# A linear-attention and MLP block on one core: attention output by tile with DMA transposes

## The chip, the cores and the metric

The kernel runs on one core of a Trainium2 chip. The metric is device time in microseconds; less is better. Engines are named as in the profile: TensorE (PE, its weight loads PEld), VectorE (DVE), ScalarE (ACT), GpSimd (POOL) and SyncE (SP), whose queue issues every DMA of this kernel.

## The reference

x has 2048 rows (tokens) of 576 bf16 values. Four layers follow one another, A, B, A, B, each added to x:

```
x = x + A(layernorm(x), wqkv, wo)      # linear attention, 32 heads of 18
x = x + B(layernorm(x), w1, b1, w2, b2)  # MLP, 576 -> 4608 -> 576

A: q, k, v = y @ wqkv;  phi(t) = where(t > 0, t + 1, exp(t)) + 1e-6
   kv = sum over tokens of phi(k)^T v,  z = sum over tokens of phi(k)   (per head)
   o = (phi(q) @ kv) / (phi(q) . z + 1e-6);   return o @ wo
B: layernorm again, h = gelu(y @ w1 + b1), return h @ w2 + b2
```

## The kernel before, in words

The tokens are 16 tiles of 128 rows. A Tile scheduler orders each engine's instructions; helper functions add dependencies that fix the order of TensorE's matmuls and of the first loads. All weights stay in SBUF. `x` between layers is kept in DRAM (`x_d`) in float32 and loaded again for each residual and layer norm.

**Layer norm** (`LNPipe`, lines 215 to 298) is a pipeline of steps, one per tick: load, statistics on VectorE (L242 to L253), rstd by a power on GpSimd (L258), the normed row tile `y_ring` on VectorE, GpSimd or ScalarE (L270, L274), for a layer B a copy of the last 64 columns beside them (L278), then five TensorE transposes (L287) into PSUM and one copy into `yT` (L289, L291). `yT` holds the transposed rows, 5 blocks of 128 columns by 2048 tokens, and every product of the layer reads it. All 64 tiles of the four layers go this way.

**Layer A, kv stage** (L348 to L403): for each tile the K projection (L356), phi on it (ScalarE exp and shift, L309 and L311, then VectorE, L312 and L314), the V projection (L364, L367) and the accumulation of kv (L380), which also sums phi(k) through a column of ones. From tile 4 on one block of Q, 126 columns by 512 tokens, is projected per tile (L386) and given phi; there are 20 blocks. In the first layer A the layer norm of the tiles runs in the same loop, as do the loads of the MLP weights; masks for the heads are built on GpSimd in the middle of it (L70 to L98).

**Layer A, output stage** (L405 on): the masked kv (L408, L412) is multiplied by `wo` for each of 5 groups of heads (L430). The denominators of 512 tokens are computed by small products (L442, L446), inverted on VectorE (L450), spread to the heads by a product (L458), copied by ScalarE (L460) and multiplied into phi(q) (L462, VectorE, some on GpSimd). Then ten products per tile give the layer's output (L470), the residual is added on VectorE (L336), stored to `x_d` (L341), and for the first four tiles the layer norm of layer B is started.

**Layer B** (`LayerB`, L516 on): in four chunks of 512 tokens. Nine groups of four hidden blocks (L569, gelu by ScalarE, L565) make the hidden layer, in which matmuls of the upper and the lower 64 rows run in pairs; then four tiles of 72 products with `w2` (L616). Residuals are fetched ahead (`prefetch_xo`), the bias is added to them on GpSimd (L326). During a chunk the layer norm of the next chunk's tiles, or at the end that of the next layer A, runs beside it; its transposes stand between the `w2` products.

SP's queue issues DMAs in order, and an instruction that waits on it holds up those behind it.

Of the kernel before, what the change touches and what calls it, by code (L numbers as in the profile page):

```python
# [14 lines left out]
S, D, F, H, DH = 2048, 576, 4608, 32, 18  # L15
P = 128
NT = S // P
KD = 5
# [17 lines left out]
def build(tc, A_x, A_wqkv, A_wo, B_w1, B_b1, B_w2, B_b2, out, dbg=None, n_layers=4):  # L36
    nc = tc.nc
    dbg = dbg or {}
    with ExitStack() as ctx:
        const = ctx.enter_context(tc.tile_pool(name="const", bufs=1))  # L40
        ps_h = ctx.enter_context(tc.tile_pool(name="ps_h", bufs=3, space=PSUM))
        ps_tp = ctx.enter_context(tc.tile_pool(name="ps_tp", bufs=1, space=PSUM))
        ps_acc = ctx.enter_context(tc.tile_pool(name="ps_acc", bufs=1, space=PSUM))
        dpool = ctx.enter_context(tc.tile_pool(name="dram", bufs=1, space=DRAM))

        x_in = A_x.flatten_outer_dims()
        out_f = out.flatten_outer_dims()

# [10 lines left out]
        maskz = const.tile([P, 7, DH], F32, name="maskz")  # L59
        head_sel = const.tile([P, G, H], BF16, name="head_sel")  # L60
        head_bc = const.tile([P, G, P], BF16, name="head_bc")
        quad_mask = const.tile([P, 4, P], BF16, name="quad_mask")
        z_row = const.tile([P, 1], BF16, name="z_row")
        eps_row = const.tile([1, H], BF16, name="eps_row")
        one_row = const.tile([1, P], BF16, name="one_row")

        def build_masks(after):
            sel = nc.gpsimd.affine_select

            def fill(tile_, value):  # L70
                tc.add_manual_dep(nc.gpsimd.memset(tile_[:], value).ins, after, NOSYNC, reason="masks are not urgent")

            fill(maskz, 1.0)
            sel(out=maskz[:], in_=maskz[:], compare_op=ALU.is_ge, fill=0.0,
                base=0, pattern=[[-DH, 7], [0, DH]], channel_multiplier=1)
            sel(out=maskz[:], in_=maskz[:], compare_op=ALU.is_ge, fill=0.0,
                base=DH - 1, pattern=[[DH, 7], [0, DH]], channel_multiplier=-1)
            sel(out=maskz[:], in_=maskz[:], compare_op=ALU.not_equal, fill=1.0,
                base=-126, pattern=[[0, 7], [0, DH]], channel_multiplier=1)
            fill(z_row, 0.0)  # L80
            fill(eps_row, 1e-6)
            fill(one_row, 1.0)
            sel(out=z_row[:], in_=z_row[:], compare_op=ALU.not_equal, fill=1.0,
                base=-126, pattern=[[0, 1]], channel_multiplier=1)
            fill(head_sel, 1.0)
            sel(out=head_sel[:], in_=head_sel[:], compare_op=ALU.is_ge, fill=0.0,
                base=0, pattern=[[126, G], [-DH, H]], channel_multiplier=1)
            sel(out=head_sel[:], in_=head_sel[:], compare_op=ALU.is_ge, fill=0.0,
                base=DH - 1, pattern=[[-126, G], [DH, H]], channel_multiplier=-1)
            fill(quad_mask, 1.0)  # L90
            sel(out=quad_mask[:], in_=quad_mask[:], compare_op=ALU.is_ge, fill=0.0,
                base=0, pattern=[[-32, 4], [0, P]], channel_multiplier=1)
            sel(out=quad_mask[:], in_=quad_mask[:], compare_op=ALU.is_ge, fill=0.0,
                base=31, pattern=[[32, 4], [0, P]], channel_multiplier=-1)
            fill(head_bc, 0.0)
            hb = head_bc[:, :, 0:126].rearrange("p g (h d) -> p g h d", h=7)
            for quad in range(4):
                sel(out=hb, in_=hb, compare_op=ALU.not_equal, fill=1.0,  # L98
                    base=-32 * quad, pattern=[[-7, G], [-1, 7], [0, DH]], channel_multiplier=1)

        wqkv_sb = const.tile([P, KD, 3 * D], BF16, name="wqkv_sb")
        wo_sb = const.tile([126, G, D], BF16, name="wo_sb")
# [4 lines left out]
        b2_bc = const.tile([P, D], BF16, name="b2_bc")  # L107
        yT = const.tile([P, KD, S], BF16, name="yT")
        kvT = const.tile([P, G, 126], BF16, name="kvT")
        zsel = const.tile([P, G, H], BF16, name="zsel")  # L110
        NY = 4
        y_ring = [const.tile([P, DPAD], BF16, name=f"y_ring{i}") for i in range(NY)]
        NV = 3
        v_ring = [const.tile([P, G, P], BF16, name=f"v_ring{i}") for i in range(NV)]
        x_d = dpool.tile([NT, P, D], F32, name="x_d")

        work = ctx.enter_context(tc.tile_pool(name="work", bufs=2))
        blk = ctx.enter_context(tc.tile_pool(name="blk", bufs=NF))

        x0_tiles = {}  # L120

        NOSYNC = mybir.DependencyInfo(mybir.DependencyClass.NoSync, mybir.DependencyReason.SCHED_ONLY)
        SYNC = mybir.DependencyInfo(mybir.DependencyClass.Sync, mybir.DependencyReason.DATA)
        relay_sb = const.tile([P, 2], F32, name="relay_sb")
        nc.gpsimd.memset(relay_sb[:], 0.0)
        chain = dict(last=None)

        def chained(inst):
            if chain["last"] is not None:
                tc.add_manual_dep(inst.ins, chain["last"], NOSYNC, reason="start-up DMA issue order")  # L130
            chain["last"] = inst.ins.name
            return inst

        pe_chain = dict(on=False, last=None)

        def pe(inst):
            if pe_chain["on"]:
                if pe_chain["last"] is not None:
                    tc.add_manual_dep(inst.ins, pe_chain["last"], NOSYNC, reason="TensorE order in the MLP")
                pe_chain["last"] = inst.ins.name  # L140
            return inst

        def load_x0(t):
            x0 = blk.tile([P, D], BF16, name="x0", tag="blk")
            chained(nc.sync.dma_start(out=x0[:], in_=x_in[t * P:(t + 1) * P, :]))
            x0_tiles[t] = x0

        def load_wqkv(part):
            cols = slice(part * D, (part + 1) * D)
            chained(nc.sync.dma_start(out=wqkv_sb[:, 0:4, cols],  # L150
                                      in_=A_wqkv[0:4 * P, cols].rearrange("(k p) n -> p k n", p=P)))
            chained(nc.sync.dma_start(out=wqkv_sb[0:64, 4, cols], in_=A_wqkv[4 * P:D, cols]))

        load_x0(0)
        load_x0(1)
        load_wqkv(1)
        load_x0(2)
        load_x0(3)
        load_wqkv(2)
        load_x0(4)  # L160
        for i in (NY - 1, 0, 1, 2):
            nc.vector.memset(y_ring[i][:], 0.0)
        warm_ps = ps_h.tile([P, 512], F32, name="warm_ps", tag="h")
        for i in range(NWARM):
            nc.tensor.matmul(warm_ps[:], lhsT=y_ring[NY - 1][:, 0:P], rhs=y_ring[NY - 1][:, 0:512], start=True, stop=True)
        act_dummy = const.tile([P, 1], F32, name="act_dummy")
        nc.scalar.activation(out=act_dummy[:, 0:1], in_=neg_half[:, 0:1], func=ACT.Exp)
        nc.vector.memset(wqkv_sb[64:P, 4, :], 0.0)
        for vr in v_ring:
            nc.gpsimd.memset(vr[:, 4, 72:126], 0.0)  # L170
            nc.gpsimd.memset(vr[:, :, 126:127], 1.0)
            nc.gpsimd.memset(vr[:, :, 127:128], 0.0)

        def late_setup():
            build_masks(pool_last["norm"])

        def piece_wo():
            chained(nc.sync.dma_start(out=wo_sb[:, 0:4, :], in_=A_wo[0:504, :].rearrange("(g p) n -> p g n", p=126)))
            chained(nc.sync.dma_start(out=wo_sb[0:72, 4, :], in_=A_wo[504:D, :]))
# [10 lines left out]
        def piece_w2(i):  # L190
            chained(nc.sync.dma_start(out=w2_sb[:, 6 * i:6 * (i + 1), :],
                                      in_=B_w2[6 * i * P:6 * (i + 1) * P, :].rearrange("(f p) d -> p f d", p=P)))
# [3 lines left out]
        def piece_b1_dma():  # L196
# [4 lines left out]

        def piece_b2_dma():
            chained(nc.sync.dma_start(out=b2_bc[:], in_=B_b2.partition_broadcast(P)))

        def bias_casts():
            nc.vector.tensor_copy(out=b1T[:], in_=bias_stage.pop("b1")[:])

        late_pieces = [piece_wo, piece_b1_dma] + [(lambda i=i: piece_w1(i)) for i in range(9)] + \
                      [(lambda i=i: piece_w2(i)) for i in range(6)]
        late_pads = [late_setup]  # L210

        state = dict(ycnt=0, vcnt=0)
        pool_last = dict(norm=None)
        dve_last = dict(norm=None)

        class LNPipe:
            def __init__(self):
# [7 lines left out]
            def busy(self):  # L225
                return len(self.items)
# [501 lines left out]
```

## Time and profile before

| | us |
|---|---|
| median of 3 runs (808.61 to 811.14) | 810.84 |
| span of the profiled execution | 809.3 |
| first layer A: kv stage and Q until the last accumulation | 0 to 77.2 |
| first layer A: output stage | 77.2 to 124.0 |
| first layer B | 124.0 to 413.4 |
| second layer A: kv stage | 413.4 to 471.3 |
| second layer A: output stage | 471.3 to 520.4 |
| second layer B and the last store | 520.4 to 809.3 |

The profile has no other time of the profiled execution than its span; the runs lie about 1.5 us above it. A row such as `L470 PE MATMUL wo_ps<-kvwo,pq 126*128 126x288 bf16 x256 | 43.8, 297` names the line, the engine, the tiles written and read, the shapes and the count, then the busy time together and the mean of one in ns. Matmuls overlap, so their mean is longer than what one adds; the chain of work gives what a run of them adds. In a row of the stretches the numbers after the length are the busy times of PE, PEld, DVE, ACT and POOL, with the count of instructions in brackets, then the granted TensorE clock, the busy share of the DMA engines and GB/s.

### The profile page before, as it was taken

The page shows a single profiled execution, that of the slowest core. Times are in us where ns is not written, and L with a number is a line of the kernel's source. Part 1 is how long each engine was busy: PE and PEld are TensorE (multiplying, and loading weights), DVE is VectorE, ACT ScalarE, POOL GpSimd, SP SyncE. Part 2 cuts the span into 40 slices and gives each one's busy share as a digit, 9 for nine tenths or more (in the row PEclk, how much of TensorE's full clock was granted, in tenths as well). Part 3 has the DMA queues.
Part 4 walks back from the last instruction along what each step waited for, and adds up shares of the span by engine and source line. Part 5 has one row for each costly group of instructions (what it writes and reads, how often), then busy time and mean ns, then how long its engine had stood idle before and what let it go on. Part 6 is the DMA issues. An engine that isn't in the chain of part 4 may idle for free.

```text
span 809.3 us, 16072 instructions
## 1 busy us (share of the span) xinstructions
PE 783.0 (97%) x6802; PEld 509.1 (63%) x6808; DVE 256.4 (32%) x714; ACT 348.8 (43%) x762; POOL 133.8 (17%) x186
## 2 busy tenths in 40 slices
PE   7999879999999999999999998899999999999998
PEld 4777554486468548745887765546854874685476
DVE  6775881034123403300344467431300300010000
ACT  4778745601630460065037786263047007404610
POOL 6981240012102201100100002120210110011000
PEclk9999999999999999999999999999999999999999
DMA  8991383011112200200110007711300120011000
GB/s 198 260 322 34 97 268 99 2 59 59 31 33 73 72 2 30 74 17 1 60 59 1 1 10 231 260 59 31 95 23 2 52 67 1 2 50 40 2 23 23
DMA packets 43649, 57.07 MB, mean 71 GB/s; under 512 B 10298, under 2 KB 28218, under 8 KB 43578
## 3 DMA queue, kind: packets, MB, share of 16 engines
q1 hardware_dynamic: 43578, 56.06, 22.9%
q8 instruction: 53, 0.87, 0.4%
q14 instruction: 18, 0.15, 0.1%
HBM read 39.53 MB, written 16.52 MB: 69 GB/s over the span
## 4 chain that ended last, share of the span: by engine, by line
PE 87%; POOL 4%; ACT 3%; DVE 2%; DMA 2%; issue 2%; SPq 0%; POOLq 0%; ACTq 0%; DVEq 0%
PE m_ps L616 35%; PE h_ps L569 19%; PE hp_ps L569 15%; PE q_ps L386 4%; PE k_ps L356 4%; PE wo_ps L470 3%; PE v_ps L367 2%; PE tp L287 2%; PE v_ps L364 2%; POOL y_ring L274 2%; ACT rden_bc L460 1%; PE kvacc L380 1%; POOL ln_rstd L258 1%; DMA wqkv_sb<-in_A_wqkv_dram 1%; DVE xn L336 1%
## 5 line engine op out<-in xcount | busy, mean ns | idle before, releaser
L616 PE MATMUL m_ps<-w_sb,hT 128*128 128x288 bf16 x2304 | 289.8, 286 | 0.0
L616 PEld LDWEIGHTS <-hT 128*128 128x128 bf16 x2304 | 223.2, 98 | 57.9 <-issue 3.4
L569 PEld LDWEIGHTS <-w_sb 64*128 64x128 bf16 x2304 | 124.5, 94 | 136.4 <-issue 1.9
L569 PE MATMUL hp_ps<-yT,w_sb 64*128 64x512 bf16 x1152 | 178.0, 376 | 0.0
L574 ACT COPY relay_sb<-relay_sb 128x1 f32<-128x1 f32 x144 | 28.5, 198 | 281.8 <-PE h_ps L569 239.2
L569 PE MATMUL h_ps<-yT,w_sb 64*128 64x512 bf16 x1152 | 147.9, 376 | 0.0
L565 ACT ACTIVATE hT<-h_ps,b1T 128x512 bf16<-128x512 f32 x144 | 91.0, 683 | 44.2 <-PE h_ps L569 44.2
L291 DVE COPY yT<-tp 128x640 bf16<-128x640 bf16 x40 | 19.6, 489 | 262.5 <-PE tp L287 262.5
L565 ACT ACTIVATE hT<-hp_ps,b1T 128x512 bf16<-128x512 f32 x144 | 91.1, 692 | 0.0
L258 POOL TENSOR_TENSOR ln_rstd<-ln_u,neg_half 128x1 f32<-128x1 f32 x64 | 35.5, 554 | 326.4 <-DVE ln_u L251 180.0
L326 POOL TENSOR_TENSOR xo<-xo,b_bc 128x576 f32<-128x576 f32 x32 | 40.9, 1278 | 181.9 <-DMA xo<-x_d 171.2
L470 PE MATMUL wo_ps<-kvwo,pq 126*128 126x288 bf16 (+1 forms) x320 | 48.2, 298 | 13.5 <-POOL pq L462 10.2
L569 PE MATMUL h_ps<-yT,w_tail 64*128 64x512 bf16 x144 | 54.1, 376 | 0.0
L569 PE MATMUL hp_ps<-yT,w_tail 64*128 64x512 bf16 x144 | 54.1, 376 | 0.0
L386 PE MATMUL q_ps<-yT,wqkv_sb 128*126 128x512 bf16 (+1 forms) x200 | 50.0, 382 | 0.5 <-ACT phi_a L311 0.5
L336 DVE TENSOR_TENSOR xbf<-m_ps,xo 128x576 bf16<-128x576 f32 x16 | 12.0, 752 | 117.4 <-PE m_ps L616 117.4
L470 PEld LDWEIGHTS <-pq 126*128 126x128 bf16 (+1 forms) x320 | 31.4, 101 | 27.9 <-POOL pq L462 11.7
L356 PE MATMUL k_ps<-wqkv_sb,yT 128*128 128x288 bf16 x320 | 45.7, 291 | 0.0
L309 ACT ACTIVATE phi_e<-k_ps 128x288 bf16<-128x288 f32 x64 | 27.2, 426 | 36.7 <-PE k_ps L356 36.7
L312 DVE TENSOR_SCALAR phi_e<-phi_e 128x288 bf16<-128x288 bf16 (+2 forms) x104 | 30.8, 297 | 31.1 <-ACT phi_e L309 30.9
L569 PEld LDWEIGHTS <-w_tail 64*128 64x128 bf16 x288 | 27.1, 94 | 17.1
L356 PEld LDWEIGHTS <-yT 128*128 128x128 bf16 x320 | 31.0, 99 | 9.3
(94 smaller groups left out, 656.0 us busy)
## 6 DMA issues: line engine op xcount, KB each, us to landing
x_d<-xn SPq DMA_DIRECT2D x48, 288.0 KB, 2.6
xo<-x_d SPq DMA_DIRECT2D x48, 288.0 KB, 3.0
xl<-x_d SPq DMA_DIRECT2D x24, 288.0 KB, 3.1
w_sb<-in_B_w_dram SPq DMA_DIRECT2D x6, 864.0 KB, 11.5
w_sb<-in_B_w_dram SPq DMA_DIRECT2D x9, 512.0 KB, 5.1
x<-in_A_x_dram SPq DMA_DIRECT2D x17, 144.0 KB, 5.3
xbf<-in_A_x_dram SPq DMA_DIRECT2D x16, 144.0 KB, 3.8
out_dram<-xbf SPq DMA_DIRECT2D x16, 144.0 KB, 1.7
```

Source lines behind the costliest of these rows:

```text
L258: nc.gpsimd.tensor_tensor(out=rstd[:], in0=it["u"][:], in1=neg_half[:], op=ALU.pow)
L309: act_last["exp"] = nc.scalar.activation(out=e[0:rows, 0:n], in_=ps_ap, func=ACT.Exp).ins.name
L312: nc.vector.tensor_scalar(out=e[0:rows, 0:n], in0=e[0:rows, 0:n], scalar1=1.0, scalar2=1e-6, op0=ALU.min, op1=ALU.add)
L326: nc.gpsimd.tensor_tensor(out=xo[:], in0=xo[:], in1=b2_bc[:], op=ALU.add)
L336: nc.vector.tensor_tensor(out=xn[:].rearrange("p (h n) -> p h n", h=2), in0=halves, in1=xo[:].rearrange("p (h n) -> p h n", h=2), op=ALU.add)
L356: pe(nc.tensor.matmul(kp[:, 0:HALF], lhsT=yT[:, k, tok], rhs=wqkv_sb[:, k, D + half * HALF: D + (half + 1) * HALF], start=(k == 0), stop=( ...
L386: pe(nc.tensor.matmul(qp[0:GR[g], :], lhsT=wqkv_sb[:, k, GO[g]:GO[g] + GR[g]], rhs=yT[:, k, c * CA:(c + 1) * CA], start=(k == 0), stop=(k ...
L470: pe(nc.tensor.matmul(wp[:, half, 0:HALF], lhsT=pq[(g, c)][0:GR[g], j * P:(j + 1) * P], rhs=kvwo[g][0:GR[g], half * HALF:(half + 1) * HALF ...
L565: act_last["gelu"] = nc.scalar.activation(out=hT[f][:, 0:CB], in_=dst[n], func=ACT.Gelu_apprx_tanh, bias=b1T[:, f:f + 1], scale=1.0).ins.name
L569: mm = pe(nc.tensor.matmul(dst[n], lhsT=wt, rhs=mv, start=(seen[n] == 0), stop=(seen[n] == 8)))
L574: relay = nc.scalar.copy(out=relay_sb[:, 1:2], in_=relay_sb[:, 0:1])
L616: pe(nc.tensor.matmul(acc[:, half, 0:HALF], lhsT=hT[f][:, j * P:(j + 1) * P], rhs=w2_sb[:, f, half * HALF:(half + 1) * HALF], start=(f == ...
```

## The change

The attention output is made per tile. kv is accumulated with a column of ones beside each head's 18 value columns (19 per head, `DV`), so that one set of five products per tile, `num_stage`, gives numerators and denominators; VectorE inverts the denominators and multiplies, the result goes through a DMA transpose into the tile's own columns of `yT`, and `wo` is applied as a plain product (`wo_stage`). Three tiles of numerators run ahead of `wo`. kv times `wo`, the denominator and broadcast products and their masks are gone.

x stays in SBUF as bf16 (`x_sb`); `x_d`, its stores and its loads are gone. 58 of the 64 row transposes of the layer norm become DMA transposes issued by SP (`transposed`); tiles 0 to 5 of the first layer stay on TensorE. Residuals of tiles 4 to 7 of each layer A go over ScalarE and GpSimd. Four groups of the next layer B's first chunk run inside the output stage, after tiles 8, 10, 12 and 14. phi of K drops ScalarE's shift: VectorE reads PSUM itself. PSUM is two pairs of banks and four single ones; `w2` comes in 12 pieces, `wq` in five by rows, padded to 128 columns per group. TensorE's order is fixed throughout. The core of the diff:

```diff
-            def den_stage(c): ...
-            def scale_stage(g, c): ...
-            def kv_wo(g): ...
+            def num_stage(t):
+                c, j = divmod(t, TPC)
+                banks = [one("num_ps") for _ in range(2)]
+                for g in range(G):
+                    mm(kv_out(lambda b, lo, hi: banks[b][:, lo:hi], g), pq[(g, c)][0:127, j * P:(j + 1) * P],
+                       kvz[0:127, g, 0:GH[g] * DV], True, True)
+                rden = work.tile([P, H], F32, name="rden", bufs=3)
+                o = y_ring[state["ycnt"] % NY]
+                state["ycnt"] += 1
+                for b, (h0, h1) in enumerate(((0, 21), (21, 32))):
+                    nd = banks[b][:, 0:(h1 - h0) * DV].rearrange("p (h c) -> p h c", c=DV)
+                    nc.vector.reciprocal(out=rden[:, h0:h1], in_=nd[:, :, DH])
+                    nc.vector.tensor_tensor(out=o[:, h0 * DH:h1 * DH].rearrange("p (h c) -> p h c", c=DH),
+                                            in0=nd[:, :, 0:DH],
+                                            in1=rden[:, h0:h1].unsqueeze(2).to_broadcast([P, h1 - h0, DH]), op=ALU.mult)
+                nc.sync.dma_start_transpose(out=yT[:, :, t * P:(t + 1) * P], in_=o[:])
             def wo_stage(t):
-                ... lhsT=pq[(g, c)] by rhs=kvwo[g], 5 groups
+                ... mm(wp[:, half, 0:HALF], yT[:, k, tok], wo_sb[:, k, ...]), 5 blocks
+                residual(li, t, wp[:, :, 0:HALF], on_pool=TPC <= t < 2 * TPC)
+                if next_kind == "B" and t < TPC:
+                    lnq.feed(t, "B", "act")
+            q_next(); q_next(); num_stage(0); q_next(); num_stage(1); q_next(); num_stage(2); q_next()
             for t in range(NT):
+                if t + 3 < NT:
+                    num_stage(t + 3)
                 wo_stage(t)
+                q_next()
+                lnq.tick()
+                if mlp is not None and t in (8, 10, 12, 14):
+                    mlp.m1_group(0, (t - 8) // 2)
+                    mlp.flush()
+            def transposed(self):
+                tok = slice(self.t * P, (self.t + 1) * P)
+                if self.transpose == "dma":
+                    nc.sync.dma_start_transpose(out=yT[:, :, tok], in_=self.y[:])
+                else:
+                    ... five TensorE transposes and a copy, as before
-        x_d = dpool.tile([NT, P, D], F32, name="x_d")
+        x_sb = const.tile([P, NT, D], BF16, name="x_sb")
+            def residual(li, t, halves, on_pool=False):
+                xo = xo_of.pop(t)[:] if t in xo_of else x_sb[:, t, :]
+                if on_pool:
+                    sums = work.tile([P, D], F32, name="sums", tag="xo", bufs=2)
+                    nc.scalar.copy(out=two(sums[:]), in_=halves)
+                    nc.gpsimd.tensor_tensor(out=x_sb[:, t, :], in0=sums[:], in1=xo, op=ALU.add)
+                    return
+                nc.vector.tensor_tensor(out=two(x_sb[:, t, :]), in0=halves, in1=two(xo), op=ALU.add)
             def k_proj(t):
-                e = exp(kp); a = kp + C1 (ScalarE); e = min(e, 1) + 1e-6; pk = max(a, e) (VectorE)
+                e = exp(kp) (ScalarE); e = min(e, 1) + 1e-6; pk = max(kp, 0) + e (VectorE, kp from PSUM)
+        TE = 6
+        norms = [Norm(t, "A", "dve" if t < 2 else "pool", "act" if t < TE else "dma", ...) for t in range(NT)]
```

751 lines of the change are left out of this document (312 added, 439 removed).

## Prediction

> **What bounds the kernel now.** I read the first part of the page first, then the busy time of each engine in six stretches that I cut at the stages of the program (kv stage and output stage of the first attention, first MLP, the same again), then the chain of work that ended last.
>
> ```profile
> PE 783.0 (97%) x6802; PEld 509.1 (63%) x6808; DVE 256.4 (32%) x714; ACT 348.8 (43%) x762; POOL 133.8 (17%) x186
> ```
> ```profile
> core 0: us, PE busy (x) PEld busy (x) DVE busy (x) ACT busy (x) POOL busy (x), PEclk, DMA share, GB/s
> 0.00:77.20 77.20, 69.89 (x556) 51.08 (x557) 51.61 (x176) 53.06 (x123) 52.28 (x68) 1.00 0.76 213
> 77.20:124.00 46.80, 38.85 (x346) 25.43 (x349) 38.42 (x98) 28.53 (x51) 12.91 (x20) 1.00 0.55 173
> 124.00:413.40 289.40, 289.40 (x2586) 182.95 (x2586) 65.75 (x162) 98.82 (x218) 31.69 (x46) 1.00 0.14 42
> 413.40:471.30 57.90, 57.90 (x471) 44.11 (x470) 29.79 (x112) 42.39 (x105) 0.55 (x1) 1.00 0.04 12
> 471.30:520.40 49.10, 41.77 (x345) 27.05 (x348) 35.22 (x91) 28.62 (x51) 8.14 (x15) 0.93 0.54 175
> 520.40:809.30 288.90, 285.22 (x2509) 178.46 (x2508) 35.56 (x79) 97.42 (x216) 28.25 (x36) 1.00 0.13 38
> ```
>
> Over the span TensorE is busy for 97%, and that average hides the point. In both MLPs (rows 3 and 6) and in the second kv stage (row 4) TensorE never pauses: there only fewer TensorE instructions help. In the output stages (rows 2 and 5) it pauses for 8.0 and 7.3 us, and VectorE is nearly as busy as it is (38.4 and 35.2 us): there the order of the small steps counts. The first stretch has 7.3 us of pauses, mostly before the first tile.
>
> The chain gives the unit prices of TensorE.
>
> ```profile
> 127.99 1.08 PE h_ps L569 x9
> 131.88 0.21 PE h_ps L569
> ...
> 176.43 0.28 PE tp L287 x5
> ...
> 466.14 1.23 PE k_ps L356 x10
> 467.37 0.54 PE v_ps L364 x5
> 467.90 0.69 PE v_ps L367 x5
> 468.59 0.26 PE kvacc L380 x5
> 468.85 2.18 PE q_ps L386 x10
> ...
> 485.07 1.23 PE wo_ps L470 x10
> ...
> 499.96 4.67 DMA xl<-x_d
> ...
> 735.16 1.18 PE h_ps L569 x9
> ...
> 805.63 0.03 DVEq L336
> ```
>
> A K projection of one tile costs 1.23 us, V 0.54 + 0.69, the kv accumulation 0.26, one Q block 1.09 (half of 2.18), a `wo` product 1.23, five row transposes 0.28, and an MLP group 3.89 (127.99 to 131.88). The last MLP chunk, with no transposes in it, lasts from 735.16 to 805.63: 70.5 us, or 281.9 for four.
>
> **The change part by part.** *Row transposes off TensorE.* 58 of 64 tiles lose their 0.28 us. In the MLPs nothing else changes on TensorE, so each becomes 281.9 us: the first was 289.4 (saves 7.5), the second 805.63 - 520.40 = 285.2 (saves 3.3). What is late next is the DMA: a transpose is started a whole chunk (70 us) before its use, so it is hidden for any plausible price. Four groups of each MLP (4 x 3.89 = 15.5 us) move into the output stage before it; I count them there, on both sides.
>
> *First kv stage.* Ten of its tiles lose 0.28 us: 2.8. It also has two stalls that the changed masks touch.
>
> ```profile
> 30.92 0.20 POOL L71 MEMSET maskz<- 128x126 f32 x1
> 36.83 3.11 POOL L98 TENSOR_SCALAR_AFFINE_SELECT head_bc<-head_bc 128x630 bf16<-128x630 bf16 x3
> 39.91 0.60 POOL L258 TENSOR_TENSOR ln_rstd<-ln_u,neg_half 128x1 f32<-128x1 f32 x1
> 43.20 0.57 POOL L258 TENSOR_TENSOR ln_rstd<-ln_u,neg_half 128x1 f32<-128x1 f32 x1
> ...
> 39.95 0.70 PE L364 MATMUL v_ps<-wqkv_sb,yT 128*128 128x252 bf16 x5 [1.88 <-DVE v_ring L371]
> 43.28 0.45 PE L287 MATMUL tp<-ident,y_ring 128*128 128x128 bf16 x5 [0.58 <-POOL y_ring L274]
> ```
>
> GpSimd builds masks from 30.92 to 39.91, 9.0 us, and the rstd of later tiles stands behind them; VectorE is held up, V of tile 7 waits 1.88 us and the transposes of tile 8 another 0.58. The new set is a mask of 133 columns with two selects, one fill of 665 columns and a small select, an estimated 2 us (the old set fills 512 and 640 columns and has nine larger selects), and the 2.5 us of stalls go. Sum 5.3: the stage ends at 71.9 where it ended at 77.2. The norm of a tile stays on GpSimd, one per 3.3 us at most (39.91 to 43.20) against 3.8 of TensorE (1.23 + 1.23 + 0.26 + 1.09), so a transpose by DMA has a few us to land; it shares the queue with a weight piece per tile, so cover is thinnest at tile 6. K's phi now leaves PSUM by VectorE alone, one 576-wide and two 288-wide steps, near the two and two it replaces; the four one-bank buffers ask it back within 3.2 us (V, accumulation, Q, half a K). I cost that at nothing; if VectorE comes late by 0.3 us per tile it is 5 us per layer. The second kv stage had one transpose on TensorE: saves 0.3.
>
> *Output stage, TensorE.* Gone are the denominators, the broadcasts of their reciprocals, and kv times wo. New are five products per tile of 4 x 133 + 76 = 608 columns; the accumulation has 576 columns in 0.26 us, so 0.28. From the last accumulation on: seven Q blocks 7.6, 16 numerators 4.5, 16 `wo` products 19.7, four MLP groups 15.5: 47.3 us. Before, with the groups added, it was 46.8 + 15.5 = 62.3 and 49.1 + 15.5 = 64.6.
>
> *Output stage, VectorE.* This sets the time, by the rows:
>
> ```profile
> L312 DVE TENSOR_SCALAR phi_e<-phi_e 126x512 bf16<-126x512 bf16 x32 | 10.5, 327 | 19.7 <-ACT phi_e L309 19.7
> L314 DVE TENSOR_TENSOR pq<-phi_a,phi_e 126x512 bf16<-126x512 bf16 x32 | 14.2, 444 | 4.3 <-ACT phi_a L311 3.7
> L336 DVE TENSOR_TENSOR xn<-wo_ps,xo 128x576 f32<-128x576 f32 x16 | 12.0, 751 | 6.6 <-PE wo_ps L470 6.4 <-issue 0.2
> L242 DVE BATCH_NORM_STATS2 ln_st<-xn 128x6 f32<-128x288 f32 x24 | 11.0, 458 | 0.5
> L248 DVE BATCH_NORM_AGGREGATE ln_mv<-ln_st 128x2 f32<-128x12 f32 x64 | 13.0, 203 | 1.0
> L253 DVE TENSOR_SCALAR ln_u<-ln_mv 128x1 f32<-128x1 f32 x32 | 4.7, 147 | 0.5
> L270 ACT ACTIVATE y_ring<-xn,ln_nmr,ln_rstd 128x576 bf16<-128x576 f32 x8 | 6.7, 866 | 4.4 <-DVE ln_nmr L262 4.4
> L408 DVE TENSOR_TENSOR kvT<-kvacc,maskz 127x504 bf16<-127x504 f32 x2 | 1.4, 675 | 0.0
> L412 DVE TENSOR_TENSOR kvT<-kvacc,maskz 127x72 bf16<-127x72 f32 x2 | 0.5, 226 | 0.0
> L450 DVE RECIPROCAL rden<-den_ps 128x128 bf16<-128x128 f32 x8 | 7.6, 947 | 0.0
> ```
>
> A numerator tile takes two reciprocals of 21 and 11 columns (at 947 / 128 = 7.4 ns each 0.24, with a fixed part of 0.35 together) and two products out of PSUM of 378 and 198 columns. The kvT rows, 675 ns for 504 and 226 for 72, give 1.04 ns a column and 0.15 fixed: 0.54 + 0.36. Sum 1.25 us. In the built program's order nine `wo` products come before the first MLP group, and the ninth needs numerator tile 8. Up to there VectorE has 9 x 1.25 = 11.3, four residuals at 0.75 (the next four go through ScalarE and GpSimd), seven Q blocks at 0.33 + 0.44, four sets of layer-norm statistics at 2 x 0.45 + 0.20 + 0.15 = 1.25, and three mask products 1.1: together 25.8 us. Add one transpose and the ninth product: 25.8 + 3.5 + 1.2 = 30.5. TensorE has only 7.6 + 12 x 0.28 + 9 x 1.23 = 22.0 there, so it pauses 8.5 us. Behind that, MLP groups fill TensorE and VectorE catches up.
>
> *The transposes by DMA.* No run of before has one. Bounds are the nearest rows, however far:
>
> ```profile
> x_d<-xn SPq DMA_DIRECT2D x48, 288.0 KB, 2.6
> w_tail<-in_B_w_dram SPq DMA_DIRECT2D x18, 32.0 KB, 4.5
> out_dram<-xbf SPq DMA_DIRECT2D x16, 144.0 KB, 1.7
> b_raw<-in_B_b_dram SPq DMA_DIRECT2D x1, 9.0 KB, 9.5
> ```
>
> One moves 160 KB in runs of 256 B. Below stands the 144 KB store, 1.7 us; above the 2-byte gather of `b_raw`, 9.5 us. The 256 B runs of `w_tail` took 4.5 us in a crowded queue, the 288 KB store 2.6. I take 3.5 from issue to landing, between the two nearest, and keep both ends. x in SBUF empties this queue in the output stage: 288 KB stores and loads go, and with them the wait of 4.67 us for `xl` in the chain (499.96), which is part of the 64.6.
>
> *The wait added on SP.* SP takes its transposes in order, and in the built order a layer-norm transpose stands ahead of the fifth, seventh and eighth numerator transposes, and of the ninth. It waits for residual, statistics, rstd, norm and pad of its tile, and on VectorE these steps are mixed with numerator and Q steps: 3.4 us to the end of the statistics, 0.6 for rstd, 0.87 for the norm on ScalarE, an estimated 1.5 for pad, negated mean and hand-offs, 6.4 in all after its `wo` product. The numerator behind it would be ready after 4.9 (that 3.4, the rest of its own steps 0.75, and the next residual, 0.75). Queued behind it are the later numerators, and TensorE waits for those. Four times 1.5, half of it under the VectorE bound: 3.6, so 12 us of pauses per output stage (bounds 4 and 22): 47.3 + 12 = 59.3. Saved: 3.0 and 5.3.
>
> *Sum.* 5.3 + 3.0 + 7.5 + 0.3 + 5.3 + 3.3 = 24.7. Against the profiled span of 809.3 that gives 784.6; the median of the runs, 810.84, lies 1.5 above the span, so **786 us**. wq, now loaded in runs of 252 and 144 B, is hidden by K and V of the first four tiles (four times 2.7 us), the added fills of paddings by GpSimd's wait for the first tile; each us by which wq is late would hold Q of tile 4, and the end, by as much.
>
> **The rivals.**
> *TensorE stays the bound.* VectorE and the DMA overlap better than I add up, 4 us of pauses per stage: 786 - 16 = 770. For it: VectorE was 82% busy in the old stage beside pauses of 17% only. Against: numerator, residual and statistics follow one another tile by tile.
> *The transposes are served slowly, one behind another: slower.* An output stage has 20 of them (16 numerators, 4 layer-norm tiles) and cannot be shorter than 20 times the service plus 3 us. It takes the time of before at 62.3 to 64.6, so the whole gain of 24.7 is gone when 20T + 3 = 59.3 + 12.4, at T = 3.4 us of service, not latency. At the 4.5 us of the `w_tail` row: 93 per stage, 34 more twice, 3 in the first kv stage: 857. For it: short runs. Against: 18 such loads stood in a full queue, so their 4.5 us is mostly waiting.
> The Trainium skill's "VectorE: DVE Perf Modes" (The three transpose paths) gives 1309 ns for one 128 x 128 block by the DMA crossbar; five in series are 6.5 us by an estimate from that page, beyond this rival's point, and the sum would be near 960. The Trainium skill's "DMA: Bandwidth & Descriptors" (Latency and other measured facts) gives 261 GB/s for such transfers, an estimate of 0.6 us for 160 KB, and then the first rival or my forecast holds. No run here shows either.
> *The queue and the PSUM buffers hold more.* 22 us of pauses per stage instead of 12: 806.
> *The MLPs keep their time.* The transposes come back as waits of TensorE for the DMA: 10.8 more, 797.
>
> **How the numbers follow.** Forecast 0.50 (778 to 796, from 8 to 17 us of pauses per stage), TensorE bound 0.17, queue and buffers 0.14, slow transposes 0.14, MLPs unchanged 0.05. The range 766 to 812 takes in all but the slow transposes and the fast end of the first rival, 0.17 left out. A measurement of this kernel tells about 0.3% from no change, 808.4 to 813.3. Faster 0.83: all cases below, less the top of the third; same 0.03; slower 0.14.
>
> **What would show it.** MLP chunks of 70.5 us with no gap; the first kv stage ending near 72; numerator tiles of 1.25 us on VectorE; a transpose landing in 2.6 to 4.5 us; in the output stages pauses of TensorE that end on a transpose or on VectorE, about 12 us each before the first MLP group. I am wrong if transposes follow each other at more than 3.4 us, if TensorE waits in the kv stages, or if the granted clock falls there (0.93 in row 5).

## The result and the profile after

| | before | after | forecast |
|---|---|---|---|
| median of 4 runs each, us | 810.35 (808.61 to 811.14) | 797.5 (795.36 to 798.46) | 786 |
| span of the profiled execution | 809.3 | 796.4 | 784.6 |

The ratio is 0.9841 (95% interval 0.9819 to 0.9863): the kernel got 1.6% faster, by about half of what was forecast (12.9 us of span instead of 24.7). The busy time of the engines over the whole span, first part of the page of after:

```profile
PE 765.2 (96%) x6416; PEld 488.8 (61%) x6416; DVE 222.7 (28%) x672; ACT 302.5 (38%) x638; POOL 132.8 (17%) x181
```

TensorE did lose work (783.0 to 765.2), but its pauses grew from 26 to 31 us. Where, the stretches of after show, cut at the same places of the program as those of before (kv stage, output stage with four MLP groups, rest of the MLP, and again):

```profile
0.00:83.90 83.90, 70.70 (x506) 48.40 (x507) 44.90 (x146) 39.88 (x81) 46.59 (x53) 0.92 0.85 209
83.90:139.90 56.00, 50.32 (x422) 29.69 (x421) 39.65 (x131) 26.82 (x50) 14.81 (x26) 1.00 0.37 72
139.90:406.20 266.30, 266.30 (x2307) 168.31 (x2307) 46.37 (x131) 88.22 (x195) 31.97 (x45) 1.00 0.10 15
406.20:463.90 57.70, 57.70 (x467) 42.49 (x465) 28.41 (x78) 34.24 (x73) 0.55 (x1) 1.00 0.02 4
463.90:526.50 62.60, 53.86 (x421) 31.84 (x421) 48.89 (x166) 26.63 (x50) 19.96 (x39) 0.95 0.43 77
526.50:796.40 269.90, 266.29 (x2304) 168.06 (x2304) 14.53 (x23) 86.69 (x193) 18.86 (x17) 1.00 0.04 12
```

| stage | before | forecast | after | off by |
|---|---|---|---|---|
| first kv stage | 77.2 | 71.9 | 83.9 | +12.0 |
| first output stage with four MLP groups | 62.3 | 59.3 | 56.0 | -3.3 |
| first MLP with its four groups (266.3 + 15.5) | 289.4 | 281.9 | 281.8 | 0 |
| second kv stage | 57.9 | 57.6 | 57.7 | 0 |
| second output stage with four MLP groups | 64.6 | 59.3 | 62.6 | +3.3 |
| second MLP with its four groups (266.3 + 15.5) | 285.2 | 281.9 | 281.8 | 0 |

The two output stages miss in opposite directions and cancel. So the whole miss is the first kv stage, which became longer than before. It is also the stage with the lowest granted clock, 0.92; the second output stage has 0.95.

VectorE's instructions in order, late in that stage (start, duration, instruction, in brackets the idle time ahead of it and what ended it):

```profile
55.00 0.82 DVE L328 SCALAR_TENSOR_TENSOR pk<-k_ps,phi_e 128x288 bf16<-128x288 f32 x2
63.59 0.18 DVE L589 CAST b1T<-b_raw 128x36 f32<-128x36 bf16 x1 [7.76 <-DMA b_raw<-in_B_b_dram]
...
64.82 0.82 DVE L328 SCALAR_TENSOR_TENSOR pk<-k_ps,phi_e 128x288 bf16<-128x288 f32 x2
```

and TensorE's at the same time:

```profile
57.65 1.39 PE L129 MATMUL v_ps<-wkv_sb,yT 128*128 128x288 bf16 x10
...
65.33 1.36 PE L129 MATMUL k_ps<-wkv_sb,yT 128*128 128x288 bf16 x5 [4.33 <-DVE pk L328]
66.49 2.61 PE L129 MATMUL v_ps<-wkv_sb,yT 128*128 128x288 bf16 x10
```

The cast of the MLP's bias b1, needed only by the MLP, stands in VectorE's queue ahead of phi of K. It waits 7.76 us for a load; phi of K stays behind it, the PSUM buffers of K are not given back, and TensorE stops for 4.33 us. Afterwards the same ten V products take 2.61 us instead of 1.39. The load is late because of SP's queue:

```profile
24.05 1.30 SPq L249 DMA_TRANSPOSE yT<-y_ring  x1
25.41 0.57 SPq L155 DMA_DIRECT2D w_sb<-in_B_w_dram  x1
26.03 1.30 SPq L158 DMA_DIRECT2D w_tail<-in_B_w_dram  x2
27.38 1.07 SPq L133 DMA_DIRECT2D x_sb<-in_A_x_dram  x2
...
56.20 1.24 SPq L249 DMA_TRANSPOSE yT<-y_ring  x1
57.49 0.57 SPq L171 DMA_DIRECT2D b_raw<-in_B_b_dram  x1
58.12 2.74 SPq L173 DMA_DIRECT2D b_bc<-in_B_b_dram  x1
```

Transposes and loads share one queue, and since a transpose waits for its layer norm, everything behind it waits too: one weight piece gets through per transpose. b1 stood right after `wo` in the list of pieces before, and stands behind the nine pieces of `w1` after; it is issued at 57.49. In the kernel before the same cast waited for nothing:

```profile
24.13 0.17 DVE L206 CAST b1T<-b_raw 128x36 f32<-128x36 bf16 x1
```

A second hole is at 28 to 38 us: the loads of x for tiles 14 and 15, at 27.38, stand behind the transpose at 24.05 as well, and VectorE's statistics wait for them, then for buffers that GpSimd holds: a holder that is no load. The waits of TensorE and of VectorE in the first stage of after (total us, times, longest):

```profile
PE k_ps L129 <- DVE pk L328: 7.7, 3, 4.3
```
```profile
DVE b1T L589 <- DMA b_raw<-in_B_b_dram: 7.8, 1, 7.8
DVE ln_st L211 <- DMA x_sb<-in_A_x_dram: 6.7, 4, 2.8
DVE ln_u L218 <- POOL ln_rstd L225: 3.5, 3, 2.6
```

### The profile page after: what moved, and what is told of

Read it like the earlier page. It is cut to its first block, busy times and chain, and to the rows that moved or that the text cites. A ratio compares the mean times of both kernels' runs of the same rounds, so it can differ in the third digit from the quotient of the medians.

```text
span 796.4 us, 15153 instructions
## 1 busy us (share of the span) xinstructions
PE 765.2 (96%) x6416; PEld 488.8 (61%) x6416; DVE 222.7 (28%) x672; ACT 302.5 (38%) x638; POOL 132.8 (17%) x181
## 4 chain that ended last, share of the span: by engine, by line
PE 83%; DVE 5%; POOL 4%; DMA 3%; issue 2%; ACT 1%; SPq 1%; POOLq 0%; DVEq 0%; ACTq 0%
PE m_ps L129 36%; PE h_ps L129 19%; PE hp_ps L129 15%; PE v_ps L129 4%; PE k_ps L129 4%; PE q_ps L129 3%; POOL y_ring L240 3%; DMA yT<-y_ring 2%; PE wo_ps L129 2%; DVE y_ring L408 1%; POOL ln_rstd L225 1%; PE kvacc L129 1%; DVE ln_st L211 1%; DMA b_raw<-in_B_b_dram 1%; DVE x_sb L305 1%
## 5 line engine op out<-in xcount | busy, mean ns | idle before, releaser
L129 PE MATMUL m_ps<-w_sb,hT 128*128 128x288 bf16 x2304 | 283.6, 286 | 0.0
L305 DVE TENSOR_TENSOR x_sb<-m_ps,xo 128x576 bf16<-128x576 f32 x32 | 24.2, 758 | 457.1 <-PE m_ps L129 457.1
L129 PEld LDWEIGHTS <-yT 128*128 128x128 bf16 x960 | 94.1, 101 | 50.2 <-issue 10.7
L295 POOL TENSOR_TENSOR xo<-x_sb,b_bc 128x576 f32<-128x576 bf16 x32 | 40.8, 1274 | 456.1 <-DVE x_sb L305 455.8
L129 PE MATMUL wo_ps<-wo_sb,yT 128*128 128x288 bf16 x320 | 47.4, 298 | 9.4 <-DMA yT<-y_ring 9.2
L211 DVE BATCH_NORM_STATS2 ln_st<-x_sb 128x6 f32<-128x288 bf16 x128 | 52.3, 439 | 7.3 <-DMA x_sb<-in_A_x_dram 6.7
L129 PE MATMUL h_ps<-yT,w_tail 64*128 64x512 bf16 x144 | 54.1, 376 | 0.0
L129 PE MATMUL hp_ps<-yT,w_tail 64*128 64x512 bf16 x144 | 54.1, 376 | 0.0
L129 PE MATMUL k_ps<-wkv_sb,yT 128*128 128x288 bf16 x320 | 45.9, 290 | 8.0 <-DVE pk L328 7.7
L129 PE MATMUL q_ps<-yT,wq_sb 128*128 128x512 bf16 x200 | 50.3, 386 | 1.4 <-DVE y_ring L408 1.4
L129 PE MATMUL v_ps<-wkv_sb,yT 128*128 128x288 bf16 x320 | 47.6, 299 | 0.0
L363 ACT ACTIVATE phi_e<-q_ps 128x512 bf16<-128x512 f32 x40 | 23.8, 596 | 26.8 <-PE q_ps L129 24.5
```

The lines of the kernel that those rows point to most:

```text
L129: return pe(nc.tensor.matmul(out_, lhsT=lhsT, rhs=rhs, start=start, stop=stop, **kw))
L211: ins = nc.vector.bn_stats(out=stt[:, h, :], in_=xt[:, h * HALF:(h + 1) * HALF])
L295: nc.gpsimd.tensor_tensor(out=xo[:], in0=x_sb[:, t, :], in1=b2_bc[:], op=ALU.add)
L305: nc.vector.tensor_tensor(out=two(x_sb[:, t, :]), in0=halves, in1=two(xo), op=ALU.add)
L363: last["exp"] = nc.scalar.activation(out=e[:, 0:CA], in_=qp[:], func=ACT.Exp).ins.name
```

## The experiments

My theory: loads held on SP behind transposes hold VectorE, and VectorE holds TensorE. The rival: GpSimd's layer norms, busy nearly without a pause from 10 to 52 us, set the pace of the stage in any case. The ratios are to the kernel before, run on the same chip beside each. "Num. 1" is the start of the first numerator product, 2 us after the kv stage's end; "out" runs from there to the end of the last `wo` product of the layer; "between" from there to the second layer's first numerator; all from the times of those products in one profiled execution of each kernel. "Clock" is the granted TensorE clock in "out 2".

| kernel | median | ratio (95%) | num. 1 | out 1 | between | out 2 | clock | rest |
|---|---|---|---|---|---|---|---|---|
| after | 797.5 | 0.9841 (0.9819, 0.9863) | 85.9 | 54.0 | 326.0 | 60.6 | 0.94 | 269.9 |
| bias early | 791.2 | 0.9765 (0.9742, 0.9788) | 81.0 | 54.1 | 325.9 | 58.6 | 0.97 | 269.9 |
| x early | 796.8 | 0.9826 (0.9804, 0.9848) | 84.6 | 54.1 | 325.9 | 60.6 | 0.94 | 269.9 |
| bias and x early | 792.1 | 0.9773 (0.9751, 0.9795) | 81.6 | 54.0 | 326.0 | 57.9 | 0.97 | 269.9 |
| bias early, norm buffers | 790.0 | 0.9743 (0.9725, 0.9761) | 80.2 | 54.2 | 325.9 | 57.6 | 1.00 | 270.1 |
| bias, x and buffers | 784.5 | 0.9681 (0.9668, 0.9694) | 73.8 | 54.0 | 326.0 | 59.7 | 0.94 | 270.0 |
| product twice | 803.0 | 0.9908 (0.9887, 0.9930) | 86.8 | 57.7 | 326.0 | 61.2 | 1.00 | 270.0 |
| norms after numerators | 801.5 | 0.9882 (0.9863, 0.9901) | 85.8 | 55.2 | 325.9 | 61.9 | 0.94 | 269.9 |
| numerators by TensorE | 798.7 | 0.9848 (0.9828, 0.9868) | 85.7 | 57.4 | 325.9 | 57.3 | 1.00 | 269.9 |
| norm transposes by TensorE | 804.2 | 0.9912 (0.9888, 0.9936) | 84.7 | 53.8 | 335.6 | 55.3 | 1.00 | 273.8 |
| three edits, norms last | 780.0 | 0.9629 (0.9606, 0.9652) | 71.6 | 54.0 | 325.9 | 55.2 | 1.00 | 269.9 |
| three edits, first chunk by TensorE | 780.4 | 0.9632 (0.9619, 0.9646) | 74.0 | 53.2 | 325.9 | 56.8 | 1.00 | 269.9 |
| all together | 777.0 | 0.9587 (0.9574, 0.9600) | 73.4 | 52.9 | 326.0 | 52.8 | 1.00 | 270.3 |

Beside these runs the kernel before had medians of 809.9 to 811.2, so a difference of about 1 us between two medians says little; the ratios allow for it.

"Out 2" differs by 3 us (57.6 to 60.6) among the first six kernels, whose instructions in that stage stand in the same order. The granted clock goes with it: 1.00 at 57.6, 0.97 at 57.9 and 58.6, 0.94 at 59.7 to 60.6. The stage in "bias early, norm buffers" and in after (columns as in the stretches):

```profile
460.30:517.90 57.60, 49.05 (x411) 29.24 (x412) 47.00 (x160) 25.01 (x47) 19.86 (x39) 1.00 0.46 84
```
```profile
465.90:526.50 60.60, 51.86 (x412) 30.95 (x412) 47.05 (x160) 24.95 (x47) 19.96 (x39) 0.94 0.45 80
```

TensorE was busy for 2.8 us more with the same products, nearly the whole 3.0. So I compare "out 2" at the same clock, with 57.6 at 1.00; that is one execution, and the medians say what the runs as a whole gained.

### The bias early

```diff
-late_pieces = [piece_wo] + [... piece_w1 x9] + [piece_biases] + ...
+late_pieces = [piece_wo, piece_biases] + [... piece_w1 x9] + ...
```

> Edit: the two bias loads go out right after wo instead of after the nine pieces of w1; nothing else changes. Theory 1 (the late load of b1 holds VectorE): the copy of b1 waited 7.76 us for its load with phi of K queued behind it, TensorE stood 4.33 us for pk and then ran at half clock for about 2.4 us; without it the first kv stage ends about 6.8 us earlier, at 77 instead of 83.9, and the time falls from 797.5 to about 791. Theory 2 (the chain of statistics, rstd and layer norm on VectorE and GpSimd with the transposes behind it sets the pace of the stage, and the wait for b1 only stands at the end of it): TensorE waits for the transposed tiles instead, and the stage ends at 82 to 84.

791.2 us, and the stage ended 4.9 us earlier. The wait for b1 is gone, but the other hole grew: the slow bias issue on SP (the 2.74 us row above, 2.55 us here) now stood ahead of the loads of x. VectorE and TensorE in this run:

```profile
32.71 0.46 DVE L211 BATCH_NORM_STATS2 ln_st<-x_sb 128x6 f32<-128x288 bf16 x1 [4.59 <-DMA x_sb<-in_A_x_dram]
```
```profile
33.58 1.36 PE L129 MATMUL k_ps<-wkv_sb,yT 128*128 128x288 bf16 x5 [4.66 <-DVE pk L328]
```

### x early, alone and with the bias

```diff
-            for u in range(6 + 2 * t, min(NT, 8 + 2 * t)):
+            for u in range(6, NT if t == 0 else 6):
                 load_x(u)
```

> Edit: the ten loads of x of the tiles 6 to 15 are all issued before the first tile, instead of two before each of the first five tiles, so that none of them stands behind a transpose on SP; the bias loads stay late. Theory 1 (loads held on SP): the statistics' waits for x of 1.49, 1.85 and 2.82 us go, and with them TensorE's two waits for pk of 2.73 and 0.63 us and about 1.6 us at a lower clock behind them: the first kv stage ends 4 to 5 us earlier, at 79 to 80, and the time is about 793. Theory 2 (GpSimd's chain sets the pace, or the wait for b1 absorbs what is won): 83 to 84, 797.

> Both edits: bias loads right after wo, all loads of x before the first tile. Theory 1 (two held loads are the whole miss of the first kv stage): the stage ends near the forecast, 72 to 73, and the time is 786, what was forecast, less 1 for the first output stage that came better and plus 3 for the second that came worse, so 786 to 788. Theory 2 (GpSimd's chain of 2.9 to 3.3 us for each tile sets the pace): 79 to 82, 793 to 796.

796.8 and 792.1: x early won nothing that its interval shows, alone or on top of the bias. Theory 1 fell in its simple form. But TensorE still waited for phi of K, not for transposed tiles, so the rival's mechanism was not there either. VectorE with x early:

```profile
30.40 0.15 DVE L218 TENSOR_SCALAR ln_u<-ln_mv 128x1 f32<-128x1 f32 x1 [1.56 <-POOL ln_rstd L225]
33.33 0.15 DVE L218 TENSOR_SCALAR ln_u<-ln_mv 128x1 f32<-128x1 f32 x1 [1.61 <-POOL ln_rstd L225]
36.40 0.15 DVE L218 TENSOR_SCALAR ln_u<-ln_mv 128x1 f32<-128x1 f32 x1 [2.64 <-POOL ln_rstd L225]
```

With x there, the statistics run ahead until their four `ln_u` buffers are full, and then advance at GpSimd's pace, with phi of K behind them: another holder in the same place.

### More norm buffers, then all three

```diff
-stt/mv/u/r = work.tile([...], F32, name="ln_st"/"ln_mv"/"ln_u"/"ln_rstd", bufs=4/6/4/6)
+stt/mv/u/r = work.tile([...], F32, name="ln_st"/"ln_mv"/"ln_u"/"ln_rstd", bufs=16)
```

> Edit: on top of the early bias loads (791.2 us, first kv stage 79.0), the small statistics tiles of the layer norms (ln_st, ln_mv, ln_u, ln_rstd) get 16 buffers each instead of 4 to 6, so that VectorE needs not wait for GpSimd before it writes the next ln_u. Theory 3 (with the loads mended, VectorE's queue is held at 27 to 37 us by ln_u, whose 4 buffers come free at GpSimd's pace of 2.9 us for a tile, phi of K stands behind it, and TensorE waits 4.7 us for pk and then runs for a while at a lower clock): the stage ends 5 to 7 us earlier, at 72 to 74, about the forecast's 71.9, and the time is 785 to 786. Rival (GpSimd's layer norms themselves set the pace, at 2.9 us for a tile up to 52 us): TensorE waits for yT in the place of pk, the stage ends at 77 to 79 and the time is 789 to 791.

> Edit: three edits together: the bias loads go out before wo (as the first of the late pieces), all ten loads of x before the first tile, and 16 buffers for each of the layer norms' small statistics tiles. Theory 4 (three holders of VectorE's queue stand in for one another: with early x loads the wait at 28 to 37 us is for ln_u behind GpSimd, 5.2 us on TensorE; with more buffers it is for x of the tiles 14 and 15, 4.5 us; so each edit alone won 0 to 1 us and all three win the whole wait): the first kv stage ends 5 to 7 us earlier than with the early bias loads alone (numerators from 74 to 76 instead of 81.0), total 784 to 787. Rival (GpSimd's layer norms, 2.9 us for a tile until 52 us, set the pace in any case): TensorE waits for yT instead, the numerators start at 79 to 81, total 789 to 791.

With the bias early and more buffers, but x late, 790.0: inside the rival's range and outside theory 3's, yet again by a held load. VectorE there:

```profile
31.81 0.46 DVE L211 BATCH_NORM_STATS2 ln_st<-x_sb 128x6 f32<-128x288 bf16 x1 [5.69 <-DMA x_sb<-in_A_x_dram]
```

With all three edits, 784.5. (The bias loads go ahead of `wo` here and not behind it, so that step is in the gain too.) TensorE's waits in the first 80 us of that run hold no `pk` any more:

```profile
PE tp L253 <- POOL y_ring L240: 3.3, 1, 3.3
PE warm_ps L129 <- DVE y_ring L184: 1.3, 1, 1.3
PE tp L253 <- POOL ln_rstd L225: 0.8, 1, 0.8
...
PE k_ps L129 <- ACT yT L255: 0.3, 1, 0.3
```

and from 20 us on it has no pause and the full clock (columns as in the stretches):

```profile
20.00:30.00 10.00, 10.00 (x93) 7.94 (x91) 10.00 (x43) 6.51 (x14) 9.69 (x7) 1.00 0.90 132
30.00:40.00 10.00, 10.00 (x81) 7.08 (x79) 6.14 (x18) 5.63 (x13) 9.69 (x10) 1.00 1.12 233
...
60.00:71.80 11.80, 11.80 (x94) 8.24 (x92) 5.74 (x17) 7.38 (x17) 0.00 (x0) 1.00 1.02 329
```

The stage ends at 71.8, where the forecast had 71.9. GpSimd is as busy as ever (9.69 of 10 us) and from 20 us on holds nobody: the rival is out. Theory 4 stands.

### VectorE in the output stages

```diff
                     nc.vector.reciprocal(out=rden[:, h0:h1], in_=nd[:, :, DH])
+                    if b == 0:
+                        nc.vector.tensor_tensor(out=o[...], in0=nd[:, :, 0:DH], in1=rden[...], op=ALU.mult)
```

> Edit: the product of the first 21 heads with the reciprocals is made twice on VectorE in every numerator tile (the same values written again), 0.5 us more of VectorE for each of the 32 tiles and nothing else. Theory A (VectorE is the bound of the output stages until the MLP's groups come in, as the prediction had it): 9 tiles x 0.5 = 4.5 us more in each of the two output stages up to the first MLP group, about 8 to 10 us in all. Theory B (the latency through SP and the DMA transposes, or TensorE, is the bound there): under 2 us for each stage, 0 to 4 in all.

5.5 us more: between the theories. The first stage grew by 3.7, less than 9 x 0.5, and at a clock of 0.97 instead of 1.00. The second grew by 0.6 against after, but its clock was 1.00 here and 0.94 there; against the 57.6 at 1.00 it grew by 3.6. So VectorE's work counts in both stages. It isn't the only bound in either: the growth stays under the work added.

### Which transposes

```diff
-                nc.sync.dma_start_transpose(out=yT[:, :, t * P:(t + 1) * P], in_=o[:])
+                # five TensorE transposes and nc.scalar.copy, one tile ahead of wo
```

> Edit: the changed kernel, but the 32 transposes of the divided numerators go through TensorE (five transposes a tile, one tile ahead of wo) and a copy by ScalarE instead of the DMA queue. Theory (VectorE and the order on SP bound the output stages until the MLP's groups come, TensorE has 6 to 9 us of pauses in each): the first output stage stays within 2 us of 56.0, the second falls by 3 to 5 from 62.6 because its pauses for the transposes go, 792 to 798 in all. Rival (TensorE bounds the stages, so that the DMA transposes are what won there): 16 x 0.28 = 4.5 us more in each, 804 to 807.

798.7, a difference that the intervals don't show. The first stage lost 3.4, more than the theory allowed. The second won 3.3, nearly all of it by the clock: 57.3 against 57.6 at 1.00. So the numerators' DMA transposes save 3.4 us in the first stage and nothing in the second, where TensorE's waits for them came with the lower clock.

```diff
-        TE = 6
+        TE = 16
-                n = Norm(t, kind, eng, "dma")
+                n = Norm(t, kind, eng, "act")
```

> Edit: the changed kernel, but all 58 layer norm transposes that it does by DMA go through TensorE and a copy by ScalarE, as in the kernel before. Theory A (the forecast's terms): 7.5 us come back in the first MLP and 3.3 in the second, 10.8 in all, and about 3 in the first kv stage: 808 to 812. Theory B (the layer norm transposes on SP are themselves what delays the numerators' transposes in the output stages, and the transposes that came back to the first kv stage fall into its waits): 10.8 in the MLPs less 4 to 6 in the output stages, 802 to 805.

6.7 us slower, inside theory B's range: "between" +9.6 and "rest" +3.9, the MLPs' price, against -5.3 in the second output stage (-2.3 at the same clock) and -1.2 until the first numerators.

This run also tests the first kv stage, for no transpose stands on SP there. b1 is issued at 39.63 and its cast waits for nothing. Yet TensorE still waited for phi of K, behind VectorE's `ln_u`:

```profile
PE k_ps L129 <- DVE pk L328: 5.3, 1, 5.3
```
```profile
DVE ln_u L218 <- POOL ln_rstd L225: 6.3, 4, 2.6
```

So the transposes on SP are not the whole cause: the `ln_u` buffers hold VectorE without them.

### What lengthens the second output stage

SP's queue in after's second output stage, layer norms (L249) among numerators (L411):

```profile
489.52 1.27 SPq L411 DMA_TRANSPOSE yT<-y_ring  x1
490.89 1.22 SPq L249 DMA_TRANSPOSE yT<-y_ring  x1
492.20 5.71 SPq L411 DMA_TRANSPOSE yT<-y_ring  x4
501.07 3.11 SPq L249 DMA_TRANSPOSE yT<-y_ring  x2
505.19 2.92 SPq L411 DMA_TRANSPOSE yT<-y_ring  x2
508.61 4.84 SPq L249 DMA_TRANSPOSE yT<-y_ring  x3
513.54 2.55 SPq L411 DMA_TRANSPOSE yT<-y_ring  x2
```

From 501 on these are norms of later MLP chunks, put there by the scheduler ahead of the last numerators. VectorE's layer norms, grouped for the first output stage and then for the second, are four against eleven:

```profile
L240 DVE TENSOR_SCALAR y_ring<-x_sb,ln_mv,ln_rstd 128x576 bf16<-128x576 bf16 x4 | 1.7, 429 | 2.2 <-DMA yT<-y_ring 1.6 <-POOL ln_rstd L225 0.6
```
```profile
L240 DVE TENSOR_SCALAR y_ring<-x_sb,ln_mv,ln_rstd 128x576 bf16<-128x576 bf16 x11 | 4.7, 428 | 5.2 <-POOL ln_rstd L225 3.1 <-DMA yT<-y_ring 2.0
```

The first edit ordered them behind the numerators:

```diff
+                    if self.kind == "B" and self.eng == "dve":
+                        tc.add_manual_dep(ins.ins, last["num"], NOSYNC, reason="numerators go first")
```

> Edit: the changed kernel, but with the statistics of every layer norm of the MLP that runs on VectorE (token tiles 4 to 15) ordered on VectorE behind the last product of numerators and reciprocals of the layer's output stage. Theory (in the second output stage the norms of the second MLP chunk stand on VectorE ahead of the last numerators and their transposes on SP ahead of the numerators' transposes): the second output stage falls from 62.6 to 56 to 58, the first stays at 56 or gains 1, and the time falls from 797.5 to 791 to 793. Rival (the stage is long because of GpSimd's residuals and bias rows or TensorE's low clock, not the norms): 0 to 1 us, 796.5 to 797.5.

801.5, slower by 4: the norms, ordered behind the last product, ran ahead of the last residuals on VectorE, and TensorE waited for the PSUM that a residual frees:

```profile
PE hp_ps L129 <- DVE x_sb L307: 4.5, 1, 4.5
```

So the same dependency was put on the last residual (`last["res"]`) on top of the three edits, beside the first chunk's transposes on TensorE, and both:

```diff
-                n = Norm(t, kind, eng, "dma")
+                n = Norm(t, kind, eng, "act" if eng == "act" else "dma")
```

> Edit: the three edits of the run with loads and buffers, and the MLP's layer norms on VectorE (token tiles 4 to 15) ordered on VectorE behind the last residual of the layer's output stage. Theory (the norms of the second MLP chunk on VectorE and SP lengthen the second output stage; ordered behind the numerators alone they stood ahead of the last residual, for which TensorE then waited 4.5 us): the second output stage falls by 3 to 4 us (from the numerators' start to the end of wo 57.6 becomes about 54), total 3 to 4 less than without this edit. Rival (the first chunk's four layer norm transposes on SP are what delays the numerators' there): within 1 us of it.

> Edit: the three edits of the run with loads and buffers, and the layer norm transposes of the first MLP chunk (token tiles 0 to 3, eight in all), which stand on SP among the numerators' transposes, go through TensorE and a ScalarE copy. Theory (an early layer norm transpose waits on SP for GpSimd's and ScalarE's chain and holds the numerators' behind it): 1 to 3 us less in the second output stage, 0 to 1 in the first, against 4 x 0.28 = 1.1 more of TensorE in each: total -2 to +1 against the run without it. Rival (these transposes cost nothing on SP): 1.1 more in each stage, +2.

> Edit: all of it: three edits of loads and buffers, the MLP's later layer norms behind the last residual, the first chunk's layer norm transposes on TensorE. If the two causes in the second output stage are separate their gains add: 4 to 6 us under the run with loads and buffers alone; if either one removes the same wait, no more than the better of the two alone.

780.0, 780.4 and 777.0, against 784.5 without them: 4.5, 4.1 and 7.6 less, each more than expected, and the gains nearly add (8.6). Part of each is the clock, 0.94 without the edits and 1.00 with them. Against the 57.6 at 1.00 the second output stage is shorter by 2.4, 0.8 and 4.8, so the two causes together cost more than one by one. With both, the 16 numerator transposes of the second layer pass SP with no layer norm among them (L415 there is L411 of after),

```profile
454.53 40.05 SPq L415 DMA_TRANSPOSE yT<-y_ring  x16
```

and in the profile the second output stage is as short as the first (52.8 and 52.9). This version beats both kernels, 0.9587 of before.

## Why the prediction was right or wrong

The time of 797.5 lies inside the stated range but outside the 778 to 796 of the forecast's own case. That the total came no further off is in part luck: the misses of the two output stages cancel, and the first kv stage went wrong by more than its whole term. Two of the prediction's own signs of being wrong came: TensorE waited in a kv stage, and the clock fell there.

**First kv stage, 5.3 saved: wrong, and this is the whole miss.** The step that failed is the sentence "I cost that at nothing" on phi of K through VectorE alone, with its price "if VectorE comes late by 0.3 us per tile". VectorE's work per tile was not the matter. It came late by whole waits: its queue is in order, and ahead of phi the statistics and the cast of b1 waited for DMAs behind transposes on SP, and `ln_u` for buffers that come free at GpSimd's pace. TensorE's waits for `pk` were 7.7 us, and its products just behind the two longest took an estimated 4.1 us more than the same products elsewhere in the stage (by the distances of their starts): 11.8 of the 12.0 us. I had seen that a transpose "shares the queue with a weight piece per tile" and asked only what that does to the transpose, not to the loads behind it; the moved bias load, the two x loads and the four `ln_u` buffers got no term. Mended, the stage ends at 71.8, which fits the sum of what the step removes (2.8 and 2.5); the parts were not taken apart. K's PSUM buffers, the thin cover named there, are what passed the delay on to TensorE.

**First output stage, 3.0 saved: right in part, too pessimistic.** 6.3 were saved. The time to the first MLP group came out, 29.6 us (83.9 to 113.5) against 30.5 worked out, and doubling a product lengthened the stage. But that agreement is partly luck: VectorE made 12 numerator tiles in that time and not nine, in 25.3 us of work, because its instructions overlap (their durations add up to 31.3). And TensorE's longest waits there end on the transposes, 3.5 us against 1.6 on VectorE:

```profile
PE wo_ps L129 <- DMA yT<-y_ring: 3.5, 4, 1.2
```

The mean durations of a numerator tile, after:

```profile
L408 DVE TENSOR_TENSOR y_ring<-num_ps,rden 128x378 bf16<-128x378 f32 x32 | 17.5, 546 | 0.4 <-ACT y_ring L236 0.4
L408 DVE TENSOR_TENSOR y_ring<-num_ps,rden 128x198 bf16<-128x198 f32 x32 | 11.2, 350 | 0.1
L407 DVE RECIPROCAL rden<-num_ps 128x21 f32<-128x21 f32 x32 | 9.1, 284 | 7.1 <-PE num_ps L129 7.1
L407 DVE RECIPROCAL rden<-num_ps 128x11 f32<-128x11 f32 x32 | 5.8, 183 | 0.0
```

1.36 us a tile against 1.25. The pauses of TensorE were 5.7 us (56.0 less 50.3) and not 12: its own work was 50.3 where I had 47.3. The 3.6 for order on SP was also summed wrongly (half of four times 1.5 is 3.0); how much of it occurred is not shown.

**Second output stage, 5.3 saved: too optimistic.** 2.0 were saved. Of the 3.3 missed, 3.0 go with the clock: 60.6 at 0.94 and 57.6 at 1.00 for the same instructions. The sum had no term for it, though the prediction names it as a sign. I also gave both stages one sum; the second holds eleven of the MLP's later layer norms on VectorE and SP, where I counted the first chunk's four tiles alone. With those norms behind the last residual it took 55.2, 2.4 less at the same clock, and the median fell by 4.5.

**MLPs, 7.5 and 3.3 saved, and second kv stage, 0.3: right,** to 0.1 us. Putting the transposes back cost 13.5 us, somewhat more than the 11.1 taken off. The rival "MLPs keep their time" gave 797, the number that came out, by a mechanism that did not occur.

**Transposes, 3.5 us each: right side, better than taken.** The DMA view of after, KB left out for transposes, median from issue to landing:

```profile
yT<-y_ring SPq DMA_TRANSPOSE x90, 2.6
```

They landed in 2.6 us, and SP issued them at 1.2 to 1.4 us each when they were ready (four in 5.71 above), far from the 3.4 us from which the slow rival decides. The Trainium skill's "VectorE: DVE Perf Modes" (The three transpose paths) would have made five blocks in series 6.5 us, by an estimate from its 1309 ns for one block. The measured 2.6 us decides against adding up that figure.

## What to carry to other kernels

An instruction that waits on an in-order queue is a wait for everything behind it: when a transfer that waits for an engine is put on a queue that also carries loads, list every load behind it, and then every instruction that stands ahead of the critical one on the engine that needs the load. Mending one such holder may win nothing, because the next one holds the same place; take them away together before calling the cause refuted. Order loads by first use, and keep work for a later stage (casts, the next chunk's norms) behind the last critical step of this one. Before you read a difference between two profiles of a stage, compare the granted clock in it: here the same instructions took 57.6 us at 1.00 and 60.6 at 0.94.

## What the runs showed of the hardware

A DMA transpose of 128 x 640 bf16 values occupied SP for 1.2 to 1.3 us to issue and landed in 2.6. A broadcast load of one row to 128 partitions held SP's queue for 2.74 us in after and 0.59 in before; the cause is open. After a wait of 4.33 us the same ten products took 2.61 us instead of 1.39, and in that stage the granted clock was 0.92. The Trainium skill's "TensorE: Matmul & The Clock Gate" (Why this matters for your kernels) warns of idle gaps over about 3 us between bursts of products; the trace agrees for this wait. Waits between 2 and 3.1 us went either way: after 2.42 us in after's second output stage the ten `wo` products took 2.58 us, but after 3.06 us in "product twice" ten V products took 1.39. After 1.85 us in "bias early, norm buffers" ten `wo` products took 1.40. So a hole can cost more than its own length: after the 4.33 us, 1.2 us more on those ten products alone.
